# Two engines' orders and one queue's order in the second network of an attention and two-FFN kernel

## The chip, the core and the metric

The kernel runs on one core of one Trainium2 chip. The metric is device time in microseconds (us), the median of several runs of the whole program; one further run was taken with the hardware profiler, and its trace is what the rows below come from. Engines are named as in the profile: PE is TensorE's matmul, DVE is VectorE, ACT is ScalarE, POOL is GpSimd, SP is SyncE, which here only issues DMAs. Each engine, and SP's queue, works through its instructions in one fixed order.

## The reference

```python
def _attn_ref(x, state):            # x (8, 8, 512, 64), state (8, 8, 32, 64)
    ...                             # two softmax reads, joined to 8 x 544 tokens of 512
def _moe_ref(x, w_gate, w_val, w_out):
    g = x @ w_gate
    silu = g * (1.0 / (1.0 + np.exp(-g)))
    return (silu * (x @ w_val) @ w_out).astype(np.float32)
def _moe2_ref(x, w_in, w_out, alpha):          # w_in 512 x 2048, w_out 2048 x 512
    h = x @ w_in
    g = np.maximum(h, 0.0) + alpha * np.minimum(h, 0.0)
    return (g @ w_out).astype(np.float32)
def reference(...):
    x = tokens(_attn_ref(x, state))            # 4352 x 512
    return _moe2_ref(_moe_ref(x))
```

The change touches only the last function, the "second network".

## The kernel before

All matmuls are in float32 made of three passes: each operand is split into a high part (rounded to float32r, a copy by ACT, `acopy`, L77) and a low part (operand less high part, a subtraction by DVE, `sub_lo`, L83), and high x high, high x low and low x high are summed in PSUM.

The second network takes two batches of 512 tokens at a time, a pair `pr` of four, and then the 256 tokens of the states. A pair has eight steps `s` (a step works on 256 of the 2048 hidden columns), so `STEPS` has 32 steps of pairs and, from `t = LAST` = 32 on, eight steps of the states.

A step of a pair (`hidden_pair`) forms four hidden blocks h00, h01, h10, h11 (two column blocks by two batches) with seven products instead of eight, a Strassen-like scheme: sums of input blocks (`x2_sums`, `x2_forms`) are multiplied by sums of weights, and DVE adds the products out of PSUM (`plus`, L911). Each block then gets its activation (`raised`): three ACT instructions (L872 to L874) and one POOL addition (L875). From the four blocks POOL makes four differences (`less`, L915), called T1 to T4 here, which with h00, h10 and h11 are the seven operands of the product with w_out, again seven products (`LINKS`, `project`). T1, T2, T3 and T4 are split into parts in the next step (`late`).

Around each of the seven products of a step stands a place, a call of `fill()`. At each place one link of the previous two steps is worked off the list `work`: six matmuls into a PSUM bank (`acc`, L1006), and then a DVE addition of that bank into a running sum (`sum`, L1017; in the first two links of each sum an ACT copy, L77). The same bank takes the next link but one, so PE must wait until that addition has read it. On PE, products (six matmuls, L903) and links (six matmuls) thus take turns. At a place a finished output block may also be handed over (`give`): a DVE addition (L1037), a DVE transpose into a tile `o` (L1041), and four stores from SP (L1044). Input sums of the next pair (`x2_sums`, L791) and their parts (`x2_forms`) are made at places too, and the sums are stored to DRAM by SP (L792) and loaded again later.

SP issues all loads: the weights of the products (`load_w2`, L759), the weights of the links (`load_wo`, L993, two DMAs of 256 KB per link), inputs, and for the states' steps `load_last`. A DMA that has to wait for its buffer, or for the tile that it stores, holds all DMAs behind it on SP.

Order: PE follows the source over the whole kernel. For the pairs' steps DVE, ACT and POOL follow the source too (`tc.manual_schedule`), and SP's order is the scheduler's. For the states' steps only PE follows the source. There `hidden_last` makes 256 hidden columns for 256 tokens (two products of twelve 128x256 matmuls), and `held` multiplies them by w_out (L1071), two entries of `work` at each place.

Of the kernel before, what the change touches and what calls it, by code (L numbers as in the profile page):

```python
# [9 lines left out]
F32R = mybir.dt.float32r  # L10
# [15 lines left out]
def attention_and_two_ffns(ctx: ExitStack, tc: tile.TileContext, x, state, w_gate, w_val,  # L26
                           w_out1, w_in2, w_out2, alpha, out):
    nc = tc.nc
# [505 lines left out]
    with tc.manual_schedule(engines={mybir.EngineType.PE}):  # L534
# [248 lines left out]
        def x2_sums(pr):  # L783

            r = {}

            def load(d, c):
                r[d, c] = x2_raw(pr, d, c)

            def sub(k, x0, x1, to):  # L790
                nc.vector.tensor_tensor(out=r[to], in0=r[x0], in1=r[x1], op=ALU.subtract)  # L791
                nc.sync.dma_start(xt2d[pr - 1][:, k], r[to])  # L792

            b00, b01, b10, b11 = [(d, c) for d in range(2) for c in range(2)]
            return {(4, 1): lambda: (load(*b00), load(*b01)), (4, 4): lambda: sub(0, b01, b00, b00),
                    (4, 5): lambda: load(*b11), (5, 1): lambda: sub(2, b11, b01, b01),
                    (5, 3): lambda: sub(1, b11, b00, b11), (5, 4): lambda: load(*b10),
                    (5, 7): lambda: sub(3, b10, b11, b10)}
# [91 lines left out]

        left = {}

        def hidden_pair(t, fill):


# [21 lines left out]
            def hi(k, o):  # L917
                acopy(form(t, k)[:, 0], o)
# [2 lines left out]
                h = form(t, k)  # L921
                sub_lo(h[:, 1], o, h[:, 0])

            def late(key):
                left.pop(key, lambda: None)()

            g = psum([P, S], "g")
            product(g, 0)
            p1 = t2([P, S], F32, "p1")
# [10 lines left out]
            product(y, 2)  # L940
            fill()
            late("t3")
            product(v, 3, start=False)
            u3 = plus(v, p1)
            h11 = plus(y, u3)
            raised(h11, 2 * s + 1, h11)
            fill()
            late("t2")
            late("t4")
            product(g, 4, start=False)  # L950
            h00 = raised(g, 2 * s, t2([P, S], F32, "h"))
            fill()
# [19 lines left out]
                less(h10, h10, h11)  # L972

            left["h10 lo"] = rest
            for k, o in (("t1", h00), ("t3", h01), ("t2", h11), ("t4", h10)):
                left[k] = lambda k=k, o=o: (hi(k, o), lo(k, o))

        acc, sums, put_in, giving, turning = {}, {}, set(), [], []

        def store(u, o):  # L980
            nq = P // Ns
# [42 lines left out]
        def give(pr, to, e):  # L1024

            d, c = 2 * e + int(to[1]), 2 * pr + int(to[2])
            r = sums[pr, to][:, e]

            def rows(t):
                return t.rearrange("p (k t q) -> p t q k", k=SC, q=32 // SC) if c < XT else t  # L1030

            def cols(t):
                return t.rearrange("p (t q k) -> p t q k", k=SC, q=32 // SC) if c < XT else t

            y = t2([P, S], F32, "y") if c < XT else r
            if to != "o00":
                nc.vector.tensor_tensor(out=cols(y), in0=rows(sums[pr, "p1"][:, e]), in1=rows(r), op=ALU.add)  # L1037
            elif c < XT:
                acopy(cols(y), rows(r))
            o = t2([P, S // 32, 32], F32, "o")  # L1040
            nc.vector.transpose(out=o.rearrange("p t n -> p (t n)"), in_=y)  # L1041
            for i in range(4):
                dst = out[c * T:c * T + S, d * P + 32 * i:d * P + 32 * i + 32]
                nc.sync.dma_start(dst.rearrange("(t r) n -> r t n", r=32), o[32 * i:32 * i + 32])  # L1044

        def give_last(pr, to, e):

# [5 lines left out]
            def turn():  # L1053
                pt = aux([P, SC, P])
                for k in range(SC):
                    nc.tensor.transpose(pt[:, k, :], r[:, k * P:(k + 1) * P], ident)
                o = t2([P, SC, P], F32, "o")
                acopy(o, pt)
                nc.sync.dma_start(out[c * T:c * T + S, d * P:(d + 1) * P].rearrange("(k p) n -> p k n", k=SC), o)

            turning.append(turn)

# [15 lines left out]
        def hidden_last(t, fill):  # L1078
            pr, s = STEPS[t]
            x, w = x2[pr], ws2.pop(t)  # L1080
            for f in range(2):
# [6 lines left out]
                                         stop=n == 11)  # L1088
                        n += 1
                m = raised(o, 2 * s + f, t2([P, S], F32, "h")[:, :NS])  # L1090
                h = hid["s", 2 * s + f] = t4([P, 2, S], F32R, "h2")
                acopy(h[:, 0, :NS], m)
                sub_lo(h[:, 1, :NS], m, h[:, 0, :NS])
                fill()

        coming = [(lambda t=t, i=i: load_w2(t, i)) for t, (pr, s) in enumerate(STEPS) if pr < B // 2
                  for i in range(4)]
# [18 lines left out]
        blk.finish(B)  # L1116

        LAST = (B // 2) * NJ2
        def step(t, pr, s):
            for n in ((t + 1,) if t == LAST - 1 else (t + 1, t + 2) if t == LAST else (t + 2,) if t > LAST else ()):  # L1120
                if n < len(STEPS):
                    load_last(n)
            if s == 1 and pr + 1 < B // 2:
                forming.update(x2_sums(pr + 1))
            if s == NJ2 - 2 and pr + 1 < B // 2:
# [3 lines left out]

            def fill():  # L1130
                places[0] += 1
                for _ in range(len(turning)):
                    turning.pop(0)()
                for _ in range(1 if t < LAST else 2):
# [21 lines left out]
                work.extend(lambda n=n, e=e, link=link: link(n, e) for n in range(len(LINKS)) for e in range(2))  # L1156

        forming, work = {}, [lambda: None for _ in range(2 * 7 + 1)]
        with tc.manual_schedule(engines={mybir.EngineType.DVE, mybir.EngineType.Activation, mybir.EngineType.Pool}):
            for t in range(LAST):  # L1160
                step(t, *STEPS[t])
            for th in left.values():
                th()
        for t in range(LAST, len(STEPS)):
            step(t, *STEPS[t])
        for th in turning + work:
            th()


# [28 lines left out]
```

## Time and profile before

| | us |
|---|---|
| median of 3 runs | 1483.83 |
| lowest and highest | 1479.69, 1485.51 |
| the profiled execution | 1478.91 |
| its span, first to last instruction | 1477.1 |
| PE busy in the span | 1379.3 |
| PE busy from 790 to 1477 us, the second network without its first steps | 638.74 |

The span is what the trace covers; the profiled execution's own time is 1.8 us more. Trace times below are counted from the span's start.

### The profile page before, as it was taken

To read this page: it belongs to the slowest core of one execution; us is meant where nothing else is said; L and a number is where in the kernel's file an instruction comes from. 1 tells how busy PE (TensorE), PEld (TensorE's weight loads), DVE (VectorE), ACT (ScalarE), POOL (GpSimd) and SP (SyncE) were. 2 spreads that over 40 slices of the span, in tenths; PEclk is the share of its full clock that TensorE was granted. 3 is DMA by queue.
4 is the path that set the end of the run, shared out by engine and by line. 5 is a ranking of instruction groups with operands and counts; after the bars stand their busy time and mean duration, and the time that the engine had idled before them with its cause. 6 is when DMAs were issued, how large, how long until landed. Compare 5 with 4: busy or idle time off the path is not lost.

```text
span 1477.1 us, 20530 instructions
## 1 busy us (share of the span) xinstructions
PE 1379.3 (93%) x7192; PEld 1067.1 (72%) x7192; DVE 1033.7 (70%) x1591; ACT 822.6 (56%) x1408; POOL 558.8 (38%) x422
## 2 busy tenths in 40 slices
PE   5799999999898999999989999999989999999897
PEld 2467776767676776778967777778777777778686
DVE  6778536678697877443756878778886788778740
ACT  6656344555655645333557566755656567655532
POOL 4432112233142322000046566545664565555611
PEclk7999999999999999999999999999999999999999
DMA  9442250676959575202264786779756987676772
GB/s 265 169 151 50 72 137 9 184 222 186 253 170 274 145 217 137 73 1 73 79 235 150 253 274 202 188 225 314 240 153 178 314 294 230 170 241 205 285 254 91
DMA packets 274224, 271.92 MB, mean 184 GB/s; under 512 B 133704, under 2 KB 198216, under 8 KB 273096
## 3 DMA queue, kind: packets, MB, share of 16 engines
q1 hardware_dynamic: 271976, 270.21, 59.1%
q8 instruction: 57, 0.93, 0.3%
q10 hardware_dynamic: 2144, 0.39, 0.2%
q14 instruction: 47, 0.39, 0.1%
HBM read 206.05 MB, written 64.49 MB: 183 GB/s over the span
## 4 chain that ended last, share of the span: by engine, by line
PE 57%; DVE 16%; ACT 10%; issue 6%; DMA 5%; POOL 4%; SPq 2%; POOLq 0%; ACTq 0%; DVEq 0%
PE acc L503 16%; PE v L472 9%; PE g L472 9%; PE acc L1006 8%; DVE h L83 6%; PE v L903 3%; PE aux L442 3%; DVE u L911 3%; PE g L903 2%; PE aux L903 2%; DMA wo<-ws2d 2%; ACT h L77 2%; DVE sum L1017 2%; ACT m L874 2%; DMA raw<-in_moe_w_out_dram 2%
## 5 line engine op out<-in xcount | busy, mean ns | idle before, releaser
L1006 PE MATMUL acc<-h,wo 128*128 128x512 f32 x1344 | 349.4, 396 | 36.5 <-DVE sum L1017 19.0
L1006 PEld LDWEIGHTS acc<-h,wo 128*128 128x128 f32 x1344 | 251.5, 190 | 101.2 <-DVE sum L1017 28.1
L503 PE MATMUL acc<-h,wp 128*128 128x512 f32 (+1 forms) x1296 | 297.1, 380 | 7.1 <-DVE h L83 3.7
L503 PEld LDWEIGHTS acc<-h,wp 128*128 128x128 f32 x1296 | 234.3, 189 | 57.7 <-DVE h L83 4.9
L875 POOL TENSOR_TENSOR u<-u,m 128x512 f32<-128x512 f32 x96 | 128.5, 1338 | 354.3 <-ACT m L874 322.7
L83 DVE TENSOR_TENSOR h<-u,h 128x512 fp32r<-128x512 f32 x160 | 159.0, 1009 | 69.4 <-ACT h L77 68.4
L472 PE MATMUL g<-a,sw 128*128 128x512 f32 x576 | 155.9, 405 | 9.7 <-ACT sw L77 5.4
L472 PEld LDWEIGHTS g<-a,sw 128*128 128x128 f32 x576 | 105.1, 190 | 71.3 <-issue 26.0
L472 PE MATMUL v<-a,sw 128*128 128x512 f32 x576 | 154.8, 405 | 0.1
L903 PE MATMUL v<-x,w 128*128 128x512 f32 x576 | 148.7, 394 | 5.0 <-DVE u L911 5.0
L872 ACT ACTIVATE m<-u 128x512 f32<-128x512 f32 x96 | 60.3, 628 | 157.8 <-DVE u L911 153.1
L1017 DVE TENSOR_TENSOR sum<-acc,sum 128x512 f32<-128x512 f32 x184 | 125.2, 681 | 27.2 <-PE acc L1006 26.9
L472 PEld LDWEIGHTS v<-a,sw 128*128 128x128 f32 x576 | 107.7, 192 | 33.8 <-issue 9.8
L903 PEld LDWEIGHTS v<-x,w 128*128 128x128 f32 x576 | 109.0, 190 | 30.0 <-DVE u L911 7.1
L83 DVE TENSOR_TENSOR h<-h,h 128x512 fp32r<-128x512 f32 (+1 forms) x80 | 77.7, 972 | 62.5 <-ACT h L77 62.0
L284 POOL TENSOR_TENSOR m<-m,raw 128x512 int32<-128x512 int32 x44 | 61.1, 1393 | 154.1 <-DVE m L276 75.2
L77 ACT ACTIVATE h<-u 128x512 fp32r<-128x512 f32 x160 | 96.6, 622 | 28.3 <-POOL u L915 28.3
L488 DVE TENSOR_TENSOR s<-s,v 128x512 f32<-128x512 f32 (+1 forms) x84 | 54.2, 645 | 81.8 <-PE v L472 68.3
L915 POOL TENSOR_TENSOR u<-u,u 128x512 f32<-128x512 f32 x64 | 103.1, 1611 | 5.0
L83 DVE TENSOR_TENSOR sw<-aux,sw 128x512 fp32r<-128x512 f32 x96 | 62.7, 683 | 56.3 <-ACT sw L77 56.3
L903 PE MATMUL aux<-x,w 128*128 128x512 f32 x384 | 101.1, 400 | 0.0
L77 ACT ACTIVATE h<-s 128x512 fp32r<-128x512 f32 (+1 forms) x84 | 50.3, 598 | 89.9 <-DVE s L488 89.7
(148 smaller groups left out, 2145.8 us busy)
## 6 DMA issues: line engine op xcount, KB each, us to landing
wo<-ws2d SPq DMA_DIRECT2D x224, 256.0 KB, 4.8
w<-w2d SPq DMA_DIRECT2D x104, 512.0 KB, 5.5
w2d<-sp SPq DMA_DIRECT2D x32, 512.0 KB, 4.0
raw<-in_moe_w_out_dram SPq DMA_DIRECT2D x14, 1024.0 KB, 5.0
x2r<-x2d SPq DMA_DIRECT2D x25, 512.0 KB, 5.8
w<-w2d SPq DMA_DIRECT2D x48, 256.0 KB, 5.1
x2d<-xo SPq DMA_DIRECT2D x32, 256.0 KB, 3.5
raw<-in_moe_w_in_dram SPq DMA_DIRECT2D x8, 1024.0 KB, 6.2
```

Source lines behind the costliest of these rows:

```text
L77: return nc.scalar.activation(o, i, AF.Copy)
L83: (eng or nc.vector).tensor_tensor(out=o, in0=src, in1=hi.bitcast(F32), op=ALU.subtract)
L284: nc.gpsimd.tensor_tensor(out=m, in0=m, in1=lo, op=ALU.add)
L472: nc.tensor.matmul(o[:, :self.n], self.lhs(f, k, a, which), self.rhs(k, c), start=(i == 0), stop=(i == last))
L488: return nc.vector.tensor_tensor(out=self.p[f], in0=self.p[f], in1=self.product(f, 1, "v"), op=ALU.mult)
L503: nc.tensor.matmul(self.acc[e][:, :self.n], wo1[f // 2][:, f % 2, a, e * P:(e + 1) * P], t[:, c, :self.n], start=(f == 0 and i == 0), stop ...
L872: nc.scalar.activation(n, src, AF.Relu, scale=-1.0)
L875: nc.gpsimd.tensor_tensor(out=out, in0=out, in1=n, op=ALU.add)
L903: nc.tensor.matmul(o, w[:, a, q], x[k][:, q, e], start=start and n == 0, stop=stop and n == 5, skip_group_check=True)
L915: nc.gpsimd.tensor_tensor(out=o, in0=x0, in1=x1, op=ALU.subtract)
L1006: nc.tensor.matmul(o, w[:, f, a, e], h[:, q], start=first and i == 0, stop=i == 5, skip_group_check=True)
L1017: nc.vector.tensor_tensor(out=r, in0=o, in1=r, op=ALU.add)
```

## The change

Three things are altered. In `hidden_pair` the split of T2 and T4 is taken apart: their two high parts (ACT) are issued before the activation of h11, their two low parts (DVE) stay where they were. Stores of results and of the input sums are no longer issued where their data is made but one to three places later (`sending`). And the manual order covers SP and the states' steps as well; there the remaining splits of the last pair's step have fixed places (`LATE`), the states' hidden blocks are split one place later (`soon`), and `load_last` has fixed places.

```diff
             def sub(k, x0, x1, to):
                 nc.vector.tensor_tensor(out=r[to], in0=r[x0], in1=r[x1], op=ALU.subtract)
-                nc.sync.dma_start(xt2d[pr - 1][:, k], r[to])
+                sending.append([3, lambda: nc.sync.dma_start(xt2d[pr - 1][:, k], r[to])])
...
             late("t3")
+            late("t2 hi")
+            late("t4 hi")
             product(v, 3, start=False)
             u3 = plus(v, p1)
             h11 = plus(y, u3)
             raised(h11, 2 * s + 1, h11)
             fill()
-            late("t2")
-            late("t4")
+            late("t2 lo")
+            late("t4 lo")
...
-            for i in range(4):
-                dst = out[c * T:c * T + S, d * P + 32 * i:d * P + 32 * i + 32]
-                nc.sync.dma_start(dst.rearrange("(t r) n -> r t n", r=32), o[32 * i:32 * i + 32])
+
+            def send():
+                for i in range(4):
+                    dst = out[c * T:c * T + S, d * P + 32 * i:d * P + 32 * i + 32]
+                    nc.sync.dma_start(dst.rearrange("(t r) n -> r t n", r=32), o[32 * i:32 * i + 32])
+
+            sending.append([2, send])
...
                 m = raised(o, 2 * s + f, t2([P, S], F32, "h")[:, :NS])
-                h = hid["s", 2 * s + f] = t4([P, 2, S], F32R, "h2")
-                acopy(h[:, 0, :NS], m)
-                sub_lo(h[:, 1, :NS], m, h[:, 0, :NS])
                 fill()
+
+                def parts(m=m, f=f):
+                    h = hid["s", 2 * s + f] = t4([P, 2, S], F32R, "h2")
+                    acopy(h[:, 0, :NS], m)
+                    sub_lo(h[:, 1, :NS], m, h[:, 0, :NS])
+
+                soon.append(parts)
...
+        LATE = {(0, 1): ("h10 hi", "h10 lo"), (0, 2): ("t1",), (1, 1): ("t3", "t2 hi", "t4 hi"),
+                (1, 2): ("t2 lo", "t4 lo")}
...
             def fill():
                 places[0] += 1
+                for e in list(sending):
+                    e[0] -= 1
+                    if not e[0]:
+                        sending.remove(e)
+                        e[1]()
+                if t == LAST - 1 and places[0] == 4:
+                    load_last(LAST)
+                if t >= LAST and places[0] == 1 and t + 2 < len(STEPS):
+                    load_last(t + 2)
+                for key in LATE.get((t - LAST, places[0]), ()):
+                    late(key)
+                for th in soon:
+                    th()
+                soon.clear()
...
-        with tc.manual_schedule(engines={mybir.EngineType.DVE, mybir.EngineType.Activation, mybir.EngineType.Pool}):
-            for t in range(LAST):
+        with tc.manual_schedule(engines={E.DVE, E.Activation, E.Pool, E.SP}):
+            for t in range(len(STEPS)):
                 step(t, *STEPS[t])
-            for th in left.values():
+            for th in soon + turning:
                 th()
-        for t in range(LAST, len(STEPS)):
-            step(t, *STEPS[t])
-        for th in turning + work:
-            th()
+            for e in sending:
+                e[1]()
+            for th in work:
+                th()
```

ACT at one of the pairs' steps (t = 2), before: the high part of T3 (a copy from u_7117), the three instructions of h11's activation, an ACT copy of a link's sum, the high parts of T2 (from u_7067) and T4 (from u_7099), and the activation of h00.

```order
L77 ACTIVATE h_1292_7193<-u_7117 128x512
L872 ACTIVATE m_7206<-u_7204 128x512
L873 ACTIVATE u_7204<-u_7204 128x512
L874 ACTIVATE m_7206<-m_7206,alpha_sb 128x512
L77 ACTIVATE sum_7220<-acc_1287_7165 128x512
L77 ACTIVATE h_1292_7193<-u_7067 128x512
L77 ACTIVATE h_1267_7076<-u_7099 128x512
L872 ACTIVATE m_7235<-g_7136 128x512
```

The same place of ACT in the changed kernel (buffer numbers differ).

```order
L77 ACTIVATE h_1292_7193<-u_7117 128x512
L77 ACTIVATE h_1292_7193<-u_7070 128x512
L77 ACTIVATE h_1264_7060<-u_7099 128x512
L872 ACTIVATE m_7208<-u_7206 128x512
L873 ACTIVATE u_7206<-u_7206 128x512
L874 ACTIVATE m_7208<-m_7208,alpha_sb 128x512
L77 ACTIVATE sum_7222<-acc_1287_7165 128x512
```

The two high parts moved in front of h11's activation, in all 31 steps that have them; the order of DVE and of POOL in the pairs' steps, and of PE everywhere, is the same in both kernels.

SP before, in the third pair's first steps: weights of products (w), stores of output blocks (out, four DMAs each) and weights of links (wo).

```order
L759 DMA w_1781_9972<-w2d_102 128x1024
L759 DMA w_1787_10016<-w2d_102 128x1024
L1044 DMA out_dram<-o_9955 32x16x32 x4
L993 DMA wo_1792_10042<-ws2d_108 128x512
L1044 DMA out_dram<-o_10035 32x16x32 x4
L993 DMA wo_1792_10042<-ws2d_109 128x512
L993 DMA wo_1793_10045<-ws2d_108 128x512
L993 DMA wo_1793_10045<-ws2d_109 128x512
L993 DMA wo_1794_10048<-ws2d_108 128x512
L993 DMA wo_1794_10048<-ws2d_109 128x512
L759 DMA w_1796_10058<-w2d_102 128x512
```

The same place of SP in the changed kernel.

```order
L759 DMA w_1781_9968<-w2d_102 128x1024
L1051 DMA out_dram<-o_9958 32x16x32 x4
L759 DMA w_1787_10016<-w2d_102 128x1024
L998 DMA wo_1792_10038<-ws2d_108 128x512
L998 DMA wo_1792_10038<-ws2d_109 128x512
L998 DMA wo_1793_10041<-ws2d_108 128x512
L998 DMA wo_1793_10041<-ws2d_109 128x512
L998 DMA wo_1794_10044<-ws2d_108 128x512
L998 DMA wo_1794_10044<-ws2d_109 128x512
L759 DMA w_1796_10054<-w2d_102 128x512
L1051 DMA out_dram<-o_10035 32x16x32 x4
```

The store of o_10035 stood between the two halves of a link's weights and now comes six DMAs later; the loads of links and of products keep their order among themselves.

DVE at the end of the pairs' steps, before: low parts (h from h or from u; in this order h10, T1, T3, T2, T4 and a block of 256 columns of the states) and link additions (sum).

```order
L83 TENSOR_TENSOR h_2225_12560<-u_12535,h_2225_12560 128x512
L1017 TENSOR_TENSOR sum_11882<-acc_2217_12497,sum_11882 128x512
L83 TENSOR_TENSOR h_2222_12537<-h_12516,h_2222_12537 128x512
L83 TENSOR_TENSOR h_2230_12592<-u_12558,h_2230_12592 128x512
L83 TENSOR_TENSOR h_2230_12592<-u_12490,h_2230_12592 128x512
L83 TENSOR_TENSOR h_2218_12507<-u_12535,h_2218_12507 128x512
L83 TENSOR_TENSOR h_2238_12631<-h_12625,h_2238_12631 128x256
L1017 TENSOR_TENSOR sum_11564<-acc_2240_12644,sum_11564 128x512
L1017 TENSOR_TENSOR sum_11564<-acc_2245_12674,sum_11564 128x512
```

The same place of DVE in the changed kernel.

```order
L83 TENSOR_TENSOR h_2225_12560<-u_12535,h_2225_12560 128x512
L1022 TENSOR_TENSOR sum_11878<-acc_2218_12500,sum_11878 128x512
L1022 TENSOR_TENSOR sum_11560<-acc_2238_12631,sum_11560 128x512
L83 TENSOR_TENSOR h_2222_12537<-h_12516,h_2222_12537 128x512
L83 TENSOR_TENSOR h_2242_12660<-h_12603,h_2242_12660 128x256
L1022 TENSOR_TENSOR sum_11560<-acc_2243_12663,sum_11560 128x512
L1022 TENSOR_TENSOR sum_11614<-acc_2238_12631,sum_11614 128x512
L83 TENSOR_TENSOR h_2250_12706<-u_12558,h_2250_12706 128x512
L83 TENSOR_TENSOR h_2251_12711<-h_12652,h_2251_12711 128x256
```

The low parts of T3, T2 and T4 no longer stand in a block in front of the link additions: two additions stand between one and the next.

## Rows read from the trace of the kernel before

**Rows 1.** The page's head.
```profile
span 1477.1 us, 20530 instructions
```

**Rows 2.** Waits of PE, 790 to 1477 us: total us, times, longest.
```profile
PE acc L1006 <- DVE sum L1017: 19.0, 19, 6.1
PE acc L1006 <- DMA wo<-ws2d: 11.6, 5, 3.8
PE acc L1006 <- ACT sum L77: 4.7, 3, 2.7
PE acc L1071 <- ACT h L77: 1.8, 1, 1.8
PE v L903 <- DVE u L911: 1.5, 3, 0.5
```

**Rows 3.** Busy times by stretch; behind the engines PEclk, DMA share, GB/s.
```profile
890.00:910.00 20.00, 19.61 (x87) 15.90 (x86) 19.07 (x24) 14.34 (x24) 12.76 (x9) 1.00 0.72 238
...
950.00:970.00 20.00, 17.27 (x69) 13.80 (x68) 16.32 (x20) 13.10 (x24) 10.71 (x9) 0.91 0.58 141
970.00:990.00 20.00, 17.28 (x68) 13.51 (x68) 12.39 (x18) 8.71 (x16) 10.44 (x7) 0.91 0.88 283
1090.00:1110.00 20.00, 16.25 (x66) 13.02 (x66) 15.62 (x22) 11.31 (x20) 11.48 (x9) 0.93 0.49 126
1310.00:1330.00 20.00, 17.15 (x68) 13.46 (x67) 11.48 (x15) 10.70 (x21) 9.62 (x7) 0.91 0.94 319
```

**Rows 4.** DVE's groups of instructions, 790 to 1400 us: the costliest.
```profile
L83 DVE TENSOR_TENSOR h<-u,h 128x512 fp32r<-128x512 f32 x149 | 147.2, 1003 | 60.4 <-ACT h L77 59.8
```

**Rows 5.** Timeline, one step: POOL, ACT, DVE and PE rows.
```profile
837.95 2.15 POOL L915 TENSOR_TENSOR u<-u,u 128x512 f32<-128x512 f32 x1
...
842.01 0.63 ACT L872 ACTIVATE m<-u 128x512 f32<-128x512 f32 x1 [5.17 <-DVE u L911]
...
843.82 1.14 ACT L77 ACTIVATE h<-u 128x512 fp32r<-128x512 f32 x2
...
844.47 1.98 DVE L83 TENSOR_TENSOR h<-u,h 128x512 fp32r<-128x512 f32 x2 [1.90 <-ACT h L77]
846.37 0.68 DVE L1017 TENSOR_TENSOR sum<-acc,sum 128x512 f32<-128x512 f32 x1
...
847.10 1.66 PE L1006 MATMUL acc<-h,wo 128*128 128x512 f32 x6 [1.03 <-DVE sum L1017]
```

**Rows 6.** Timeline, a step with input forms: DVE at the same place.
```profile
864.00 1.29 DVE L83 TENSOR_TENSOR h<-u,h 128x512 fp32r<-128x512 f32 x2 [2.85 <-ACT h L77]
```

**Rows 7.** Timeline, a step with ACT copies of sums: ACT and PE.
```profile
952.70 0.57 ACT L77 ACTIVATE sum<-acc 128x512 f32<-128x512 f32 x1
...
953.33 2.59 PE L1006 MATMUL acc<-h,wo 128*128 128x512 f32 x6 [2.73 <-ACT sum L77]
```

**Rows 8.** SP's waits from 790 us on (first row), and a timeline around one.
```profile
SPq L1044 <- DVE o L1041: 111.6, 24, 8.6
...
1142.09 0.71 DVE L1041 STREAM_TRANSPOSE o<-sum 128x512 f32<-128x512 f32 x1
...
1142.83 1.97 SPq L1044 DMA_DIRECT2D out_dram<-o  x4
...
1145.44 2.90 SPq L993 DMA_DIRECT2D wo<-ws2d  x6
...
1149.96 1.22 PE L1006 MATMUL acc<-h,wo 128*128 128x512 f32 x4 [2.31 <-DMA wo<-ws2d]
```

**Rows 9.** Timeline, start and end of the states' steps: DVE, PE, ACT.
```profile
1398.34 1.20 DVE L83 TENSOR_TENSOR h<-u,h 128x512 fp32r<-128x512 f32 x1 [1.82 <-ACT h L77]
...
1400.63 1.28 DVE L1017 TENSOR_TENSOR sum<-acc,sum 128x512 f32<-128x512 f32 x2
...
1401.37 2.93 PE L1006 MATMUL acc<-h,wo 128*128 128x512 f32 x6 [6.10 <-DVE sum L1017]
...
1459.67 0.51 ACT L874 ACTIVATE m<-m,alpha_sb 128x256 f32<-128x256 f32 x1
```

More of the change, by code (lines that the diff above doesn't have):

```diff
@@ L891, in attention_and_two_ffns, with late @@
         left = {}
+        def late(key):
+            left.pop(key, lambda: None)()
         def hidden_pair(t, fill):
@@ L922, in lo @@
                 sub_lo(h[:, 1], o, h[:, 0])
-            def late(key):
-                left.pop(key, lambda: None)()
             g = psum([P, S], "g")
@@ L974, in hidden_pair @@
             left["h10 lo"] = rest
-            for k, o in (("t1", h00), ("t3", h01), ("t2", h11), ("t4", h10)):
+            for k, o in (("t1", h00), ("t3", h01)):
                 left[k] = lambda k=k, o=o: (hi(k, o), lo(k, o))
-        acc, sums, put_in, giving, turning = {}, {}, set(), [], []
+            for k, o in (("t2", h11), ("t4", h10)):
+                left[k + " hi"] = lambda k=k, o=o: hi(k, o)
+                left[k + " lo"] = lambda k=k, o=o: lo(k, o)
+        acc, sums, put_in, giving, turning, sending, soon = {}, {}, set(), [], [], [], []
         def store(u, o):
@@ L1058, in turn @@
                 acopy(o, pt)
-                nc.sync.dma_start(out[c * T:c * T + S, d * P:(d + 1) * P].rearrange("(k p) n -> p k n", k=SC), o)
+                sending.append([1, lambda: nc.sync.dma_start(
+                    out[c * T:c * T + S, d * P:(d + 1) * P].rearrange("(k p) n -> p k n", k=SC), o)])
             turning.append(turn)
@@ L1118, in attention_and_two_ffns @@
         LAST = (B // 2) * NJ2
+        LATE = {(0, 1): ("h10 hi", "h10 lo"), (0, 2): ("t1",), (1, 1): ("t3", "t2 hi", "t4 hi"),
+                (1, 2): ("t2 lo", "t4 lo")}
         def step(t, pr, s):
-            for n in ((t + 1,) if t == LAST - 1 else (t + 1, t + 2) if t == LAST else (t + 2,) if t > LAST else ()):
-                if n < len(STEPS):
-                    load_last(n)
+            if t == LAST:
+                load_last(t + 1)
             if s == 1 and pr + 1 < B // 2:
@@ L1158, in attention_and_two_ffns @@
         forming, work = {}, [lambda: None for _ in range(2 * 7 + 1)]
-        with tc.manual_schedule(engines={mybir.EngineType.DVE, mybir.EngineType.Activation, mybir.EngineType.Pool}):
-            for t in range(LAST):
+        E = mybir.EngineType
+        with tc.manual_schedule(engines={E.DVE, E.Activation, E.Pool, E.SP}):
+            for t in range(len(STEPS)):
                 step(t, *STEPS[t])
-            for th in left.values():
+            for th in soon + turning:
                 th()
-        for t in range(LAST, len(STEPS)):
-            step(t, *STEPS[t])
-        for th in turning + work:
-            th()
+            for e in sending:
+                e[1]()
+            for th in work:
+                th()
 _INS = ['x', 'state', 'moe_w_gate', 'moe_w_val', 'moe_w_out', 'moe2_w_in', 'moe2_w_out', 'moe2_alpha']
```

## The prediction

> **What bounds the kernel now.** I began with the page's head: one execution of 1477.1 us from first to last instruction [rows 1], and 1478.91 us as a whole. The changed kernel does the same work on PE in the same order, so what it can win is PE's waiting in the second network, and what can be lost is new waiting there. The second view is therefore the list of PE's waits from 790 us on [rows 2]: 19.0 us for DVE's link additions (of which one single wait of 6.1), 11.6 us for link weights, 4.7 us for ACT's copies of link sums, 1.5 us for DVE's additions of products, 1.8 us near the end. That is 38.6 us, 2.6% of the span. The third view is the busy time by stretch [rows 3]: in four of the five stretches PE's granted clock is on average 0.91 to 0.93 of full speed, and each of these holds one of the long waits. In the fifth, at full speed, 87 matmuls took 19.61 us, 0.225 each. By that the 69, 68, 66 and 68 matmuls of the four would need 15.6, 15.3, 14.9 and 15.3 us; they took 17.27, 17.28, 16.25 and 17.15. So the long waits cost a further 6.9 us behind themselves, and the wait at 1401.37, whose six matmuls took 2.93 us [rows 9] where 1.66 is usual behind a short wait [rows 5], another 1.3: 8.2 us in sum.
>
> The fourth view is the timeline around these waits, to see what is late. At 847.10 PE waits 1.03 us for a link addition [rows 5]. DVE did that addition at 846.37, right behind the low parts of T2 and T4, and it had stood still for 1.90 us in front of these, waiting for their high parts on ACT. ACT made them at 843.82, behind h11's activation, which it could begin only at 842.01 because it had itself waited 5.17 us for h11. T4, the last of the four differences, was ready on POOL at 837.95 + 2.15 = 840.10. So ACT stood idle with the work ready, and then did it last. It is the rule, not an accident: from 790 to 1400 us DVE waited 59.8 us for ACT in front of these subtractions [rows 4], about 2 us in each of some 30 steps, 1.90 where nothing else is in the way and 2.85 where ACT also has an input form to copy [rows 6].
>
> The fifth view is SP's own waits: 111.6 us in 24 cases for the transposed tile `o` of a store [rows 8]. Around 1142 us one sees what that does: `o` is made at 1142.09, the four stores are issued at 1142.83 and take 1.97 us, the six link loads behind them go out from 1145.44, and PE, which needs the first of them, has waited 2.31 us when it starts at 1149.96.
>
> **High parts of T2 and T4 first.** The move adds no instruction: two ACT copies, 1.14 us together [rows 5], go from behind h11's activation into ACT's wait in front of it (5.17 us there). DVE's wait of 1.9 to 2.85 us in front of the low parts then goes, as far as POOL has T4 ready. In [rows 5] there are 842.01 - 840.10 = 1.9 us for a copy of some 0.6, so it is hidden completely. With that wait gone DVE reaches its next link addition about 1.9 us sooner, which is more than any wait of PE on such an addition but the 6.1 of the states' steps. The waits that hang on it: 19.0 - 6.1 = 12.9 for additions, 1.5 for sums of products, 4.7 for ACT's copies, 19.1 in all [rows 2]. I don't count them whole. In the wait at 953.33 the copy at 952.70 stood in a row of ACT's work that is hardly idle in these steps, so of its 2.73 us [rows 7] I let 1.0 stay, and of the rest another 1.6, since in the steps with input forms DVE is nearly full. Gain: 16.5, at least 8 (half of it), at most 19.1.
>
> A rule speaks against counting it even so. DVE's subtractions of this place come earlier, nearer to POOL's differences. What a row shows of the two engines side by side: the two low parts took 1.98 us beside a POOL addition [rows 5] and 1.29 without one [rows 6], so 0.69 us for the pair, a third of the wait that goes. With that price in every step DVE still gains 1.2 us or more. The Trainium skill (SBUF — State Buffer, section "Who interferes with whom") says that a DVE instruction with two SBUF inputs and a GpSimd instruction that reads SBUF contend for a shared port pair, which one holds for its whole instruction while the other is blocked; by it each of the two subtractions could lose a whole POOL difference, and this part of the gain would be gone.
>
> **Stores later.** Again nothing is added. A store of a block comes two places later, each of a product and a link, 2 x 12 x 0.225 = 5.4 us, so its tile has long been made when SP comes to it, and link loads no longer wait behind DVE. What this holds up: tile `o` is kept longer; a change of two places in a buffer cycle of about a step (seven places) I price at nothing, and at one wait of 2 us per pair if ACT should need the buffer, 6 us, for the range. Stores of input sums come three places later; they are loaded again two places after that or later, and SP would wait there for a landing, which I also price at nothing. The 11.6 us for link weights lie at four places, and three of them lose the store in front of their loads in the new order. At the fourth, around 1145 us, a store still stands right in front of the six loads. It was held up by the same late DVE (1.9 us) and PE comes earlier as well, so I let 1.4 of its 2.31 us stay. Gain: 10.2; nothing at the worst, 11.6 at the most.
>
> **The states' steps.** The 6.10 us wait at 1401.37 is for additions that DVE did at 1400.63, behind a block of low parts, the last but one of which waited for ACT until 1398.34 [rows 9]. In the new order two additions stand between one low part and the next, the wait goes, and I find nothing that brings it back: 6.1. Two small things are added. A block of the states is split one place later, so ACT does the next block's activation first: three instructions of up to 0.51 us [rows 9] ahead of it, and in the last step but one, where its operands are used at once, PE has room for about half of that and waits some 0.9 us. And a transpose of an output block follows directly on its last addition, 0.9. Net gain 4.3; nothing to 6.1.
>
> **The clock.** The waits of 2.7 us and more lie in the slow stretches, that of 2.31 [rows 8] in none of them. If they go or become short, the 8.2 us go too; I count 7.0, and 2 if most of the long waits stay.
>
> Sum: 16.5 + 10.2 + 4.3 + 7.0 = 38.0 us, from 1478.9 to 1440.9 us for an execution like the profiled one. The median of the runs shown is 4.9 us above that execution, so a median of the changed kernel should be near 1445. Everything together, with nothing new, is 38.6 + 8.2 = 47 us, or 1437 by the median: the floor, with 3 us of spread among runs 1434.
>
> **The rivals.** Times are by the median.
>
> *DVE is the next bound.* In the steps with input forms it has the most to do, and if PE no longer waits it may have no room. For it: in one of these stretches, from 890 to 910 us, DVE is busy 19.07 of 20 us [rows 3]. Against it: PE is busy 19.61 us in the same stretch, so the two just keep pace, and 59.8 us of DVE's waiting come free [rows 4]. Then 8 us of waits stay: 1453.
>
> *Link loads stay late.* Not the stores but the landing and full DMA engines (share 0.88 and 0.94 in two of the stretches [rows 3]) make them late. Against it: at 1145.44 the loads went out late by SP's order alone. Then 10.2 us and 5 of the clock stay: 1460.
>
> *DVE and POOL block each other.* The low parts now meet POOL's differences, at more than the 0.69 us shown. It decides at the 1.9 us that the pair gains; then the first part goes (16.5) with 2 of the clock: 1464. The rule cited above would have it so.
>
> *It does nothing.* ACT waits for T4 instead of DVE for ACT, and stores only change place: within 0.5%, 1476 to 1491.
>
> *Slower: ACT held by POOL.* The copy of T4 now stands in front of h11's activation, so ACT, and with it the copies of sums, the activations of h00 and h10 and the products' PSUM banks, wait whenever POOL's four differences end late. The room is 1.9 us in [rows 5] less the copy of 0.6. If POOL's chain ended so late that each of the 31 steps lost 1.5 us more on PE, 46 us would be lost and 38 won: 1491. It costs from where T4 comes 1.3 us later than in that row, and eats the whole gain from 1.3 + 38 / 31 = 2.5 us later. POOL's difference there took 2.15 us already, so there is little reason for it.
>
> **How the numbers follow.** I give the forecast 0.68, DVE as bound 0.08, late loads 0.12, blocking 0.04, nothing 0.04, slower 0.04. The predicted time is the forecast's, 1445 us. Its own range is 1434 to 1452. The range to 1463 takes in DVE as bound and late loads, 0.88 together with the forecast; that leaves out blocking and the last two. A change of 0.5%, 7.4 us, is about what a measurement of this kernel can tell from none: faster 0.68 + 0.08 + 0.12 + 0.04 = 0.92, same 0.04, slower 0.04.
>
> **What would show it.** In the new profile DVE's wait for ACT in front of the subtractions of [rows 4] should fall from 59.8 to under 20 us, and PE's waits for additions from 19.0 to under 5. SP's waits for `o` should be nearly gone, and PE's for link weights under 3 us. The clock should be at full speed in all stretches from 950 to 1400 us. At the states' steps there should be no wait over 2 us. The prediction would be wrong if PE waited as long as before for another releaser (POOL through ACT, above all), or if waits went and PE's busy time did not fall with them.

## The result, and the profile after

The changed kernel took 1431.44 us (median of 4 runs, 1427.95 to 1434.24), the kernel before 1484.67 (4 runs, 1479.69 to 1489.48): a ratio of 0.9641, 95% interval 0.9599 to 0.9682. The gain of 53 us has the forecast sign but not the forecast size: 1445 was predicted, 1434 to 1463 as its range, so the time lies 2.6 us below it, and even below 1437, which the prediction called the floor.

The page's head, and PE's waits from 790 us on, to be set beside [rows 1, 2]:

```profile
span 1432.1 us, 20515 instructions
...
PE acc L1081 <- ACT h L77: 2.2, 2, 1.4
PE acc L1011 <- ACT sum L77: 1.3, 2, 0.9
PE aux L1065 <- DVE sum L1022: 1.3, 1, 1.3
PE acc L1011 <- DVE sum L1022: 0.3, 1, 0.3
PE aux L1065 <- DVE sum L1060: 0.2, 1, 0.2
```

Of 39.2 us in 33 waits (38.6 in the 31 of [rows 2], and two short ones of 0.6 together), 5.3 us in 7 are left. The waits for link weights are gone altogether, those for link additions have fallen from 19.0 us to 0.3, with one of 1.3 at a new place, in front of a transpose.

Busy times in the five stretches of [rows 3]:

```profile
890.00:910.00 20.00, 20.00 (x90) 16.55 (x89) 19.20 (x25) 15.67 (x26) 13.48 (x9) 1.00 0.75 251
950.00:970.00 20.00, 19.74 (x87) 15.89 (x86) 19.65 (x22) 13.64 (x24) 11.78 (x8) 1.00 0.66 174
970.00:990.00 20.00, 20.00 (x90) 16.57 (x89) 15.71 (x23) 14.39 (x26) 14.32 (x11) 1.00 1.01 340
1090.00:1110.00 20.00, 20.00 (x90) 16.53 (x90) 14.29 (x18) 15.63 (x29) 11.63 (x9) 1.00 0.74 214
1310.00:1330.00 20.00, 20.00 (x90) 16.57 (x89) 16.93 (x22) 13.76 (x24) 12.27 (x9) 1.00 0.59 199
```

The granted clock is full in all of them, and PE makes 87 to 90 matmuls where it made 66 to 87. In one of them DVE is busy 19.65 of 20 us and PE still hardly waits, which also answers the first rival: DVE is close to its limit, and not over it.

DVE's low parts (790 to 1400 us), and SP's waits for the tiles of stores, to be set beside [rows 4, 8]:

```profile
L83 DVE TENSOR_TENSOR h<-u,h 128x512 fp32r<-128x512 f32 x150 | 138.8, 941 | 19.5 <-ACT h L77 19.2
...
SPq L1051 <- DVE o L1046: 86.7, 23, 7.7
```

DVE's wait for ACT in front of these subtractions fell from 59.8 to 19.2 us, as forecast. SP's waits for `o` fell only from 111.6 to 86.7, where "nearly gone" was forecast, and yet PE waits for no link weights: the reason given for that term was wrong (below).

One step of the changed kernel, timeline of ACT, DVE, PE and POOL:

```profile
842.32 0.64 ACT L77 ACTIVATE h<-u 128x512 fp32r<-128x512 f32 x1 [1.06 <-POOL u L918]
...
845.21 0.68 DVE L1022 TENSOR_TENSOR sum<-acc,sum 128x512 f32<-128x512 f32 x1
845.33 0.63 ACT L872 ACTIVATE m<-u 128x512 f32<-128x512 f32 x1 [2.38 <-DVE u L914]
845.81 1.28 DVE L83 TENSOR_TENSOR h<-u,h 128x512 fp32r<-128x512 f32 x2
845.87 1.52 PE L906 MATMUL v<-x,w 128*128 128x512 f32 x6
...
847.01 0.68 DVE L1022 TENSOR_TENSOR sum<-acc,sum 128x512 f32<-128x512 f32 x1
847.23 1.52 PE L1011 MATMUL acc<-h,wo 128*128 128x512 f32 x6
847.32 1.30 POOL L875 TENSOR_TENSOR u<-u,m 128x512 f32<-128x512 f32 x1 [5.04 <-ACT m L874]
...
848.59 1.52 PE L906 MATMUL aux<-x,w 128*128 128x512 f32 x6
```

ACT waits 1.06 us for POOL's difference, makes the high part at 842.32, and still waits 2.38 us for h11, so the copies cost it nothing. DVE does the two low parts without a wait in front, in 1.28 us instead of 1.98, and PE's groups start every 1.36 us. The 1.28 us are worth a look: POOL does nothing from the end of T4 until 847.32, so the pair now has no POOL instruction beside it. In the kernel before, it had this one (the pair began at 844.47, [rows 5]):

```profile
844.00 1.30 POOL L875 TENSOR_TENSOR u<-u,m 128x512 f32<-128x512 f32 x1 [3.90 <-ACT m L874]
```

The executions do not begin the second network at the same time. Its first product starts at 742.31 us in the profile before and at 747.85 in this one, because the clock was lower in the first 180 us: 0.94 of full speed on average before, 0.91 in this one. So I compare from that first product to the last instruction: 1477.1 - 742.31 = 734.8 us before, 1432.1 - 747.85 = 684.3 after. The second network gained 50.5 us, against 38.0 in the forecast's sum.

### The profile page after: what moved, and what is told of

Same layout as the page of the kernel before. It is cut to its first block, busy times and chain, and to the rows that moved or that the text cites. A ratio compares the mean times of both kernels' runs of the same rounds, so it can differ in the third digit from the quotient of the medians.

```text
span 1432.1 us, 20515 instructions
## 1 busy us (share of the span) xinstructions
PE 1369.7 (96%) x7192; PEld 1067.8 (75%) x7192; DVE 1029.4 (72%) x1591; ACT 827.6 (58%) x1408; POOL 554.9 (39%) x422
## 4 chain that ended last, share of the span: by engine, by line
PE 75%; DVE 7%; DMA 4%; ACT 4%; issue 4%; POOL 4%; SPq 0%; ACTq 0%; POOLq 0%; DVEq 0%
PE acc L1011 17%; PE acc L503 16%; PE v L472 9%; PE g L472 9%; PE v L906 7%; PE g L906 5%; PE aux L906 5%; PE aux L442 3%; DMA raw<-in_moe_w_out_dram 2%; POOL u L918 2%; PE acc L1081 1%; DVE h L83 1%; POOL u L875 1%; DMA wo<-ws2d 1%; DVE sw L83 1%
## 5 line engine op out<-in xcount | busy, mean ns | idle before, releaser
L1011 PE MATMUL acc<-h,wo 128*128 128x512 f32 x1344 | 341.4, 390 | 2.5 <-ACT sum L77 1.3
L83 DVE TENSOR_TENSOR h<-u,h 128x512 fp32r<-128x512 f32 x160 | 148.8, 946 | 24.6 <-ACT h L77 24.1
L77 ACT ACTIVATE h<-u 128x512 fp32r<-128x512 f32 x160 | 100.5, 630 | 91.3 <-POOL u L918 90.1
L83 DVE TENSOR_TENSOR h<-h,h 128x512 fp32r<-128x512 f32 (+1 forms) x80 | 79.3, 993 | 49.4 <-ACT h L77 49.2
L906 PE MATMUL g<-x,w 128*128 128x512 f32 x384 | 98.4, 392 | 1.4 <-ACT h L873 1.4
L874 ACT ACTIVATE m<-m,alpha_sb 128x512 f32<-128x512 f32 (+1 forms) x144 | 99.2, 689 | 0.0
```

Of the source, the lines that this page charges most:

```text
L77: return nc.scalar.activation(o, i, AF.Copy)
L83: (eng or nc.vector).tensor_tensor(out=o, in0=src, in1=hi.bitcast(F32), op=ALU.subtract)
L874: nc.scalar.activation(n, n, AF.Copy, scale=alpha_sb[:, f:f + 1])
L906: nc.tensor.matmul(o, w[:, a, q], x[k][:, q, e], start=start and n == 0, stop=stop and n == 5, skip_group_check=True)
L1011: nc.tensor.matmul(o, w[:, f, a, e], h[:, q], start=first and i == 0, stop=i == 5, skip_group_check=True)
```

## The experiments

Each is named by its label. "Second network" is the time just defined. Each ratio is to runs of the kernel before that were made together with it.

**e1_t2t4_back**, the changed kernel with the first part undone:

```diff
-            late("t2 hi")
-            late("t4 hi")
...
-            late("t2 lo")
-            late("t4 lo")
+            late("t2 hi")
+            late("t2 lo")
+            late("t4 hi")
+            late("t4 lo")
...
```

and the same order in `LATE`.

> The changed kernel with T2's and T4's high parts back behind h11's activation; stores and states' steps stay changed. From the start of the second network to the last instruction the kernel before takes 734.8 us, the changed one 684.3. Theory: DVE waits for ACT again in front of the low parts (19 us in the changed kernel, 60 before), and PE's waits for additions, sums of products and ACT's copies come back, 19.1 us in 25 waits where 1.6 in 3 are left now; each costs 0.3 us beyond its listed idle time, because the matmuls before and behind it no longer overlap, so 17.5 + 22 x 0.3 + one slow stretch of the clock (1.7) = about 26 us: 710 us. If a wait costs only its listed time: 704. Rival, that SP's order and the later stores had also made these waits: under 5 us, 689.

1464.34 us, ratio 0.9872 (0.9843 to 0.9901); second network 717.1, 32.8 more than the changed kernel. PE's waits, and three groups around one of them:

```profile
PE acc L1011 <- DVE sum L1022: 13.6, 18, 1.7
...
PE acc L1011 <- ACT sum L77: 4.9, 3, 2.8
```
```profile
847.01 1.52 PE L906 MATMUL aux<-x,w 128*128 128x512 f32 x6
849.55 1.66 PE L1011 MATMUL acc<-h,wo 128*128 128x512 f32 x6 [1.02 <-DVE sum L1022]
851.05 1.54 PE L906 MATMUL g<-x,w 128*128 128x512 f32 x6
852.43 0.84 PE L1011 MATMUL acc<-h,wo 128*128 128x512 f32 x3
```

The theory's waits came back, the rival (under 5 us more) falls, and the theory's size was nearer than that of the listed time alone (710 and 704 expected), though 7 us too small: 20.5 us of listed waits came back instead of 17.5, and two slow stretches of the clock instead of one. The four rows show what a wait costs. From 847.01 to 852.43 three groups took 5.42 us, where three regular ones take 3 x 1.36 = 4.08: lost are 1.34 us, listed is a wait of 1.02. The rest is not listed as idle: the group before the wait is listed with 1.52 us although a regular successor would start after 1.36, and the group behind it takes 1.66. A wait of 0.20 us costs as much beside itself:

```profile
870.11 1.52 PE L906 MATMUL g<-x,w 128*128 128x512 f32 x6
871.83 1.65 PE L1011 MATMUL acc<-h,wo 128*128 128x512 f32 x6 [0.20 <-DVE sum L1022]
873.32 1.52 PE L906 MATMUL v<-x,w 128*128 128x512 f32 x6
```

From 870.11 to 873.32 two groups took 3.21 us, 0.49 more than two regular ones.

**e2_stores_at_once**, the changed kernel with stores where their data is made:

```diff
-            sending.append([2, send])
+            send()
```

and the same for the stores of input sums and of the states' steps.

> The changed kernel with every store issued where its data is made; SP still follows the source, T2 and T4 stay early. Theory: the later stores are what removed PE's waits for link weights; 11.6 us in 5 waits come back with 1.5 beyond their listed time and three slow stretches of the clock (5.1): about +18 us, 702 us in the second network. Rival: SP still waits 86.7 us for the tiles of stores in the changed kernel (111.6 before), so the places did little, and it was the earlier DVE that made the tiles in time: under +4 us, 684 to 688.

1470.82 us, ratio 0.9914 (0.9889 to 0.9939); second network 725.4, 41.1 more. PE's waits, SP's for `o`, and the timeline of one of them:

```profile
PE acc L1011 <- DMA wo<-ws2d: 28.3, 10, 6.7
...
SPq L1051 <- DVE o L1046: 119.2, 22, 13.7
```
```profile
1302.50 0.71 DVE L1046 STREAM_TRANSPOSE o<-sum 128x512 f32<-128x512 f32 x1
1303.24 1.94 SPq L1051 DMA_DIRECT2D out_dram<-o  x4
...
1305.83 2.99 SPq L998 DMA_DIRECT2D wo<-ws2d  x6
...
1310.82 1.22 PE L1011 MATMUL acc<-h,wo 128*128 128x512 f32 x2 [6.02 <-DMA wo<-ws2d]
```

The rival falls: with T2 and T4 early, DVE's tiles are still not early enough. But my +18 was too small as well. The order of the kernel before is not this one with the stores at once: in its trace several stores are issued behind loads that follow them in the source. SP in strict source order, without the later places, costs more than the old order did: with T2 and T4 early and the old order (e5 below) PE waits 9.3 us for link weights, here 28.3.

**e3_states_back**, the changed kernel with the states' steps as before: `for t in range(LAST)` in the manual order, no `LATE`, no `soon`, `load_last` at a step's start.

> The changed kernel with the states' steps as before: not in source order on DVE, ACT, POOL and SP, remaining splits in one block at the end of the pairs' steps, blocks of the states split at once, weights loaded at the step's start. Theory: the 6.1 us wait for an addition behind the block of low parts comes back with its slow clock (1.3), and the changed order's own waits there (1.27, 0.75, 1.45) go while the 1.8 near the end returns: +5 to +7 us, 690 us in the second network. Rival: with T2 and T4 early DVE gets through the block in time, so the wait does not return: 682 to 684, the states' steps then gave nothing or cost something.

1436.96 us, ratio 0.9681 (0.9656 to 0.9706); second network 690.5, 6.2 more, inside the theory's range. One row says it:

```profile
PE acc L1011 <- DVE sum L1022: 5.3, 1, 5.3
```

The wait of the states' steps stays at 5.3 us although T2 and T4 are early: it hangs on the order there.

**e4_changed_again**, the changed kernel unaltered:

> The changed kernel once more, to see what two executions differ by. Every theory: the second network takes 684 us again within 1, and what differs is the time before its start (742.3 us in the profile before, 747.9 in the changed one), where the clock was half for 20.5 and 30.7 us. If the second network differs by more than 2 us, the comparison of single profiles is not good enough.

1435.25 us (1431.67 to 1436.90), ratio 0.9667 (0.9641 to 0.9694). The second network took 685.0 us, 0.7 from the first profile; it began at 749.8. Differences of single profiles in the second network are thus good to about 1 us. Of the 2.7 us between these two executions 1.9 lie ahead of it.

**e5_t2t4_alone**, the kernel before with only the first part of the change's diff.

> The kernel before with T2's and T4's high parts in front of h11's activation and nothing else changed. In the changed kernel this move was worth 32.5 us (717.1 to 684.3 in the second network from its start to the last instruction); the kernel before takes 734.8. Theory A, the parts add up: about 702 us, PE's waits for link weights stay near 11.6. Theory B, the parts need each other: PE without its waits for additions comes to its link weights sooner, stores at their old places hold the loads up more often (10 waits of 28.3 us with stores at once and in source order), so link weights cost 15 us and more and the move alone gives 10 to 25 us: 710 to 725 us.

1453.39 us, ratio 0.9795 (0.9777 to 0.9813); second network 704.8, near theory A's 702 and outside theory B's 710 to 725. PE's waits:

```profile
PE acc L1011 <- DMA wo<-ws2d: 9.3, 3, 4.2
PE acc L1011 <- DVE sum L1022: 5.6, 2, 5.3
```

The move alone gives 30.0 us. All additions that PE still waits for are one of 5.3 at the states' steps and one of 0.3, and link weights cost 9.3 instead of 11.6.

**e6_stores_alone**, the kernel before with `sending` and SP in source order for the pairs' steps.

> The kernel before with only the stores one to three places later and SP in source order for the pairs' steps; T2, T4 and the states' steps as before. Both theories: waits for link weights near 1 us, and all waits for additions and copies stay (19.0 and 4.7 us). With T2 and T4 late but the states' steps changed it was 717.1 us; the old states' steps cost about 6 more, so 723 us. If later stores are worth as much alone as in the changed kernel (41 us against stores at once), it would be under 700; the theory excludes it, since the order of the kernel before lies between.

1468.42 us, ratio 0.9901 (0.9876 to 0.9925); second network 721.8, as expected. PE's waits:

```profile
PE acc L1011 <- DVE sum L1022: 19.0, 19, 6.0
...
PE acc L1011 <- DMA wo<-ws2d: 1.4, 2, 0.7
```

Later stores, with SP's order that goes with them, give 13.0 us alone and leave the waits for additions as they were. The parts add up: 30.0 + 13.0 + 6.2 for the states' steps (e3) are 49.2 of the 50.5.

**e7_one_place** and **e11_four_places**, the changed kernel with other delays:

```diff
-            sending.append([2, send])
+            sending.append([1, send])      # e7
+            sending.append([4, send])      # e11
```

In e7 the stores of input sums come one place later too; in e11 they stay at three.

> The changed kernel with all stores one place later instead of two and three. Theory: what counts is how many matmuls lie between a load's place behind the store and its use; at once gives 725.4 us, two and three places 684.3, one place lies between, 690 to 705, with some of PE's waits for link weights back (5 to 15 us). Rival, that it is only SP's waiting for the tile: SP waits 119 us at once and 87 in the changed kernel, so most of its wait never went and one place should give nearly the whole gain, 684 to 688.

> The changed kernel with stores of results four places later instead of two (those of input sums stay at three). Theory: what counts is which loads stand behind a store; with two places none of PE's waits is for link weights any more, so four give nothing: 684 to 686 us in the second network, though SP's waits for the tiles fall from 87 us to 50 or less. Rival, that a longer kept tile holds up ACT or DVE (a tile cycle of about seven places): 688 or more.

| places of result stores | SP waits for `o` | PE waits for link weights | second network | median, ratio |
|---|---|---|---|---|
| 0 (e2) | 119.2 | 28.3 | 725.4 | 1470.82, 0.9914 |
| 1 (e7) | 99.4 | 10.1 | 698.3 | 1444.66, 0.9745 (0.9723 to 0.9768) |
| 2 (changed) | 86.7 | none | 684.3 | 1431.44, 0.9641 |
| 4 (e11) | 50.1 | none | 684.5 | 1430.60, 0.9651 (0.9631 to 0.9671) |

Both rivals fall. SP's wait for the tile and PE's wait for the weights are two different things: from two to four places the one loses 37 us and the time stays.

**e8_both_ends** tries to better the changed kernel: two projections of the first network go into the first steps of the second, and the last steps are rearranged.

```diff
+        work[9], work[11] = lambda: blk.project(NF1 - 2), lambda: blk.finish(B)
...
-                for _ in range(1 if t < LAST else 2):
+                for _ in range(1 if t < LAST or t >= len(STEPS) - 2 else 2):
```

> The changed kernel with its own remaining waits attacked: the last two projections of the first network are put into the second network's empty places in front of its two longest starting waits (2.07 and 1.42 us listed, 5.5 and 3.5 lost from start to start); transposes of output blocks two places after their addition instead of one; one piece of work instead of two at each place of the last two steps, and the last step's block split at once. Theory, by start-to-start losses: 3 us from the beginning (2 x 1.4 of matmuls moved into waiting), 1.6 from the 1.27 us wait for an addition, 2 to 3 from the two waits of 0.75 and 1.45: the second network less what moved into it about 6 us shorter, 1426 us where the changed kernel is 1432. Rival: the holes at the start are not for want of work but hold back the same chain on DVE, which then only starts later: 2 to 3 us.

1428.47 us (1426.72 to 1432.10), ratio 0.9632 (0.9611 to 0.9653): the interval overlaps that of the changed kernel, so a gain is not told apart. The waits at the end went, but a new one came. SP's wait and the timeline behind it:

```profile
SPq L512 <- DVE xo L80: 39.3, 1, 39.3
...
769.69 3.88 SPq L512 DMA_DIRECT2D x2d<-xo  x4
...
774.17 3.02 SPq L998 DMA_DIRECT2D wo<-ws2d  x6
...
778.87 2.93 PE L1011 MATMUL acc<-h,wo 128*128 128x512 f32 x6 [4.39 <-DMA wo<-ws2d]
```

The moved store of `xo` holds SP for 39.3 us, and the link loads behind it come late: the lesson of e2 at another place.

**e9_ends_other_queue**, e8 with those stores issued by ACT (`blk.finish(B, nc.scalar)`).

> The kernel of e8 with the first network's last four stores issued by ACT instead of SP. In e8 SP waited 39.3 us for the first of their tiles, the link loads behind it went out from 774.17 us, PE waited 4.39 us for them (7.15 lost from start to start) and the clock was half for one stretch more (1.7). Theory: off SP's queue nothing is held up, so e8's 685.6 us in the second network become 676 to 678, and with the start at 744.8 the execution 1421 to 1424 us by the median, faster than the changed kernel by 8 to 11. Rival: the loads are late because they also wait for tiles that the two moved projections keep: 683 to 686, no better than e8.

1430.08 us (1426.11 to 1431.15), ratio 0.9646 (0.9626 to 0.9666). The second network, the two moved projections in it, took 684.3 us: not the theory's 676 to 678, and inside the rival's range, but not for the rival's reason. The wait for link weights went, but at the same place PE now waited 1.8 us for ACT's and 0.9 for DVE's part of a hidden block. It looks as if in the first steps that chain were the bound, and work moved in only filled its holes; no run tests it. Neither kernel is shown to beat the changed one.

**e10_slow_dve**, the changed kernel with T2's low part done twice and T4's three times (the result is the same):

```diff
-                left[k + " lo"] = lambda k=k, o=o: lo(k, o)
+                left[k + " lo"] = lambda k=k, o=o: [lo(k, o) for _ in range(2 if k == "t2" else 3)]
```

> The changed kernel with three low parts done again in each of the 31 steps (T2's once, T4's twice more), some 2.9 us more of DVE in front of a link addition, so that PE waits for additions as often as before or more. It measures what a wait costs. Theory: the second network grows by the listed idle time, 0.3 us for each wait that is added, and 1.7 us for each added slow stretch of the clock; with some 30 to 60 waits more, 9 to 18 us beyond the listed time and the clock. Rival: a wait costs what is listed, and what was won beyond it came from elsewhere: within 2 us of the listed time and the clock.

1510.53 us in one run; second network 764.1, 79.8 more than the changed kernel. PE's waits, and two stretches of busy time:

```profile
PE acc L1011 <- DVE sum L1022: 38.4, 26, 3.6
PE v L906 <- DVE u L914: 10.8, 8, 3.0
PE acc L1011 <- ACT sum L77: 4.7, 3, 2.9
```
```profile
845.00:865.00 20.00, 16.55 (x65) 13.19 (x66) 17.14 (x23) 11.14 (x20) 11.58 (x8) 0.91 0.75 246
865.00:885.00 20.00, 19.76 (x87) 16.06 (x86) 17.95 (x23) 13.34 (x22) 9.40 (x7) 1.00 0.82 274
```

Listed waits rose from 11.1 us in 12 to 61.5 in 47. The clock, as the sum of (1 - PEclk) x 20 us over stretches like these, cost 19.8 us where it cost 1.8. Those are 50.4 + 18.0 = 68.4 of the 79.8; 11.4 us are left over for 35 more waits, 0.33 each. The rival, which allowed 2 us, falls.

## Why the prediction was wrong

The direction was right, and each of the three parts took away a little more listed waiting than forecast (17.5, 11.6 and 4.8 us for 16.5, 10.2 and 4.3). The step that failed is the sum's unit: every term for a wait was the listed idle time of PE, and "everything together, with nothing new, is 38.6 + 8.2 = 47 us" took these, with the clock, for the whole cost of the waits. A term is missing from it, some 0.3 us for each wait besides its listed time (its restart, below). That the time fell just outside the range is partly chance: the same kernel took 1435.25 us in e4, inside it. The size was missed either way, by 10 to 14 us. The same account over ten kernels, from the second network's first product on (waits as PE's list has them, the clock worked out as in e10, without the end, where PE has finished; it overstates where a slow stretch falls into a wait):

| kernel | second network | waits (number) | clock | remainder |
|---|---|---|---|---|
| before | 734.8 | 45.7 (38) | 12.2 | 676.9 |
| e6, stores alone | 721.8 | 35.6 (35) | 9.0 | 677.2 |
| e1, T2 and T4 back | 717.1 | 31.6 (34) | 5.2 | 680.3 |
| e2, stores at once | 725.4 | 39.3 (21) | 15.8 | 670.3 |
| e7, one place | 698.3 | 20.5 (15) | 7.0 | 670.8 |
| e5, T2 and T4 alone | 704.8 | 24.4 (14) | 12.1 | 668.3 |
| changed | 684.3 | 11.1 (12) | 1.8 | 671.4 |
| e11, four places | 684.5 | 11.2 (12) | 1.8 | 671.5 |
| e3, states back | 690.5 | 15.0 (10) | 6.8 | 668.7 |
| e10, slow DVE | 764.1 | 61.5 (47) | 19.8 | 682.8 |

The remainder ought to be the same, since PE's work is. It isn't: it grows with the number of waits, by 0.35 us for each (a line through the ten; standard error 0.05). From start to start the rows of e1 give 0.32 and 0.29, and e10, which was made to test it, 0.33. Part of it could have been expected. The Trainium skill (TensorE: Matmul & The Clock Gate, "Single matmul latency" and "Back-to-back issue gap") gives, for a single bf16 matmul of 512 columns at full clock, a latency of (398 + 512) / 2.4 = 379 ns, and for an isolated matmul a gap to the next of 512 / 2.4 + 2.5 = 216 ns. Their difference, an estimate of 0.16 us by that page, is what a matmul gives up when no other follows at once. The trace agrees for the group in front (1.52 less 1.36 us); the further 0.14 of the group behind (1.66 less 1.52) isn't in that figure.

Point by point, in listed time:

- **T2 and T4 first**: 16.5 forecast. Of the 19.1 us counted, 1.6 are left (0.3 for additions, 1.3 for ACT's copies): 17.5, and 0.7 more in the steps ahead of 790 us that I had not counted. The mechanism is right (e1, e5). Measured with what hangs on it, the restart of 20 and more waits and the clock, the move is worth 30 to 33 us.
- **Stores later**: 10.2 forecast, 11.6 gone; alone worth 13.0 with its share of restarts and clock. The size is right and the reason half wrong. I wrote that a tile "has long been made when SP comes to it"; SP still comes before the tile is made and waits 86.7 us. What the delay changes is which loads stand behind the waiting store: those that PE needs two places later. The table of places bears that out; that nothing else of the order changed with it was not shown.
- **The states' steps**: 4.3 forecast, 4.8 found: 6.10, 1.76 and two short waits of 0.54 together went, and 3.64 came. The two small costs that I named did appear, 1.27 for the transpose and 0.75 for the later split, and a third that I had missed, 1.45 us at the end, where the last block's split is late for the same reason:

```profile
1359.67 0.65 PE L1065 MATMUL aux<-ident,sum 128*128 128x128 f32 x4 [1.27 <-DVE sum L1022]
...
1414.02 2.67 PE L1081 MATMUL acc<-wo,h 128*128 128x512 f32 x9 [0.75 <-ACT h L77]
...
1419.57 3.41 PE L1081 MATMUL acc<-wo,h 128*128 128x512 f32 x12 [1.45 <-ACT h L77]
```

- **The clock**: 7.0 forecast of 8.2; all of it came back, no stretch from 790 us to PE's last matmul is slow.
- **The 4.9 us** added to get a median was about right: the second network's start lay between 742.3 and 749.8 us in the profiles, and that of before lay lowest.

So of the 12.5 us that the sum fell short in the second network, 34.6 + 8.2 - 38.0 = 4.8 are allowances for waits that did not stay, and some 26 x 0.3 = 8 are the restarts of 26 waits. The table divides the same 50.5 us otherwise: 34.6 of waits, 10.4 of clock and 5.5 of remainder. Its clock column is the one that overstates, so the restarts' share of the miss is known to 2 or 3 us only.

The rivals: DVE is not the next bound, though busy 98% in one stretch. Link loads do not stay late: PE waits for none, though the DMA engines' share is 1.01 from 970 to 990 us. With the stores nearer than two places they are late (e2, e7), so it was SP's order that decided. ACT is not held by POOL to its cost.

Work of DVE beside POOL does cost time, but less than before, and here I had the direction wrong. I feared that earlier low parts would meet POOL's differences. T4 is the last of these, so the pair that waits for it comes behind them, and in the step shown above it now falls into POOL's idle time (1.28 us), where it ran beside POOL's addition before (1.98). Over all low parts of [rows 4] the mean fell from 1003 to 941 ns. The contention itself is still there in single rows of the changed kernel: one low part takes 0.68 us with POOL idle and 1.37 beside an addition.

```profile
843.29 0.68 DVE L83 TENSOR_TENSOR h<-u,h 128x512 fp32r<-128x512 f32 x1
...
848.90 1.30 POOL L875 TENSOR_TENSOR h<-h,m 128x512 f32<-128x512 f32 x1 [0.27 <-ACT m L874]
...
849.38 1.37 DVE L83 TENSOR_TENSOR h<-u,h 128x512 fp32r<-128x512 f32 x1 [1.08 <-ACT h L77]
```

The Trainium skill (SBUF — State Buffer, "Who interferes with whom") says that a DVE instruction with two SBUF inputs contends with a GpSimd instruction that reads SBUF. These rows agree with it; what failed is my premise that the move brings the two together.

## What to carry to other kernels

Price a wait of PE from start to start of the groups around it, not by its listed idle time: here each cost 0.3 us more, a quarter of the mean wait before (45.7 us in 38), and that was the largest part of the miss. On a queue that works in order, ask not how long an instruction waits there but which transfers stand behind it and when they are needed; a store belongs as many places later as lie between its data and the loads that it must not hold. And an engine's idle time in front of its other input (ACT in front of h11) is the place for copies that a third engine waits for.

## What the runs showed of the hardware

- A break in PE's stream costs about 0.3 us besides the listed wait: 0.16 of overlap lost in front and 0.14 behind (e1's rows), 0.35 (standard error 0.05) over ten kernels, and 0.29 when the wait itself is only 0.20 us (e1).
- The clock was lower where PE waited long. In e10 the granted clock was 0.91 in the stretch around a wait of 2.83 us, and over the second network low clock cost 19.8 us; in the changed kernel, from 790 to 1400 us, it was 1.00 throughout.
- Low parts on DVE lose time beside POOL's work: two took 1.98 us beside an addition in the kernel before and 1.28 without one in the changed kernel.
- What lies ahead of the second network varies: it began at 742.3 to 749.8 us in the profiles, while its own length repeated within 1 us in the two profiles of the changed kernel (684.3 and 685.0).
